# Attention with a two-layer network on one core: the lower parts of the first layer's results may go to VectorE or GpSimd in every group, and two of the attention's products get a wider planning margin

## Chip, cores and metric

One core of a Trainium2 chip. The metric is device time in microseconds, the median of the runs shown. The inputs are the reference's; the program is compiled with its whole order fixed, so what can change from one version to the next is which engine does an operation and where it stands in that engine's queue.

## What is computed

```python
# q, k, v: (4, 8, 768, 64); n_global = 8, n_local = 96
scores = scale * np.matmul(q, k.transpose(0, 1, 3, 2))
keep = is_global | is_local            # first 8 keys, and the last 96 up to the query
bias = -slopes[:, None, None] * dist[None, :, :]
scores = np.where(keep, scores + bias, -1000000000.0)
a = softmax(scores)                    # maximum, exp, sum + 1e-9
x = np.matmul(a, v).transpose(0, 2, 1, 3).reshape(3072, 512)
h = x @ w_in                           # 512 -> 2048
g = np.where(h > 0.0, h, np.exp(np.minimum(h, 0.0)) - 1.0)
out = g @ w_out                        # 2048 -> 512
```

## The kernel before

The 3072 rows are twelve **groups** of 256 rows (four batches of three). Each group has an attention part and a network part. The attention of a group is four **pairs** of heads (`pair`). In the groups 4 to 11 each head goes through `head`: for each of its two tiles of 128 queries a score product `s` (line 561), the softmax on VectorE and ScalarE (`pr`, lines 478, 480, 487, 488, 468), the transposes of the weights `t` (line 575), their split into a rounded upper half and the rest (`pt`, ScalarE line 287 and VectorE line 295), and the product with the values `pv` (line 587). Then VectorE adds the two halves to `x` (line 459), and `xh` and `xl` are the upper and lower parts of the group's rows. There is one bank for `t` and one for `pv`: the next transposes wait until VectorE has read the last `t`. The groups 0 to 3 take another way (`heads32`), which the change does not touch.

The network of a group is `moe`: for each of 16 slices of the hidden width, `up` makes h with twelve products of 256 columns (line 606), ScalarE and VectorE apply the nonlinearity (lines 612 to 614), ScalarE rounds it to the upper part `gh` (line 615, helper line 287), and the **lower part** `gl = e - gh` is a subtraction (line 616, helper line 295). `down` adds six products of 512 columns to the group's two outputs `o` (line 628): four with gh, two with gl. TensorE works on the network of one group while the attention of the next is prepared beside it.

The order of all this is no loop but a plan. `Plan.add` records each operation with the engines that may do it and their estimated costs (`dve(W, port=True)` is VectorE, `pool(W)` is GpSimd; `port` says that the operation takes the memory port that the two share), a due time, and a `slack`. `Plan.order` goes through them greedily: it takes, per engine, first what is ready, by due time. An operation with several engines is only given to one if no other would end sooner. The slack is a margin: an operation counts as ready only `slack` after its inputs from other engines,

```python
t = t + self.SEM + op.slack if of != e else t - self.LAT["PE"] if e == "PE" else t
at = max(at, f + self.SEM + 0.3 * op.slack)
```

and 0.3 of it after its buffer came free (second line). So a wider margin makes the plan put other work in between; the program itself waits on semaphores alone and does not add the margin. Before, the margin is 600 ns for the score products, the transposes and the value products of `head`. The subtraction for `gl` may go to either engine in the groups 0 to 2 and in the last group, and to GpSimd alone in the groups 3 to 10.

Of the kernel before, what the change touches and what calls it, by code (L numbers as in the profile page):

```python
# [20 lines left out]
W = NT * P  # L21
# [180 lines left out]
def pe(cols):  # L202
    return (("PE", cols * 0.47, False),)


def act(n, psum=False, extra=0.0):
    return (("ACT", (55 if psum else 97) + 0.834 * n + extra, False),)


def dve(n, fast=False, port=False):  # L210
    return (("DVE", (75 + 0.521 * n) if fast else (70 + 1.042 * n), fast or port),)


def pool(n, two=True):
    return (("POOL", (30 + 2.58 * n) if two else (50 + 1.1 * n), True),)


def sp():
    return (("SP", 450.0, False),)
# [21 lines left out]
class Kernel:  # L241
# [306 lines left out]
    def head(self, b, h, t0, j, qd, ql, ks, vd, pv, due, step):  # L548

        nc, p, slack = self.nc, self.plan, self.SLACK  # L550
        st = self.sb("st", "st", [P, 3, NT])
        prs = []
        for i in range(NT):
            lo = 0 if t0 + i else P
            n, c0 = 2 * P - lo, NG + i * (NG + P) + lo
            s = self.bank("s", "s", [P, 1, 2 * P])
            prs.append(self.sb("pr", "pr", [P, 2 * P]))

            def scores(e, i=i, s=s, lo=lo, n=n, c0=c0):
                for m, x in enumerate((qd, ql)):  # L560
                    nc.tensor.matmul(s.t[:, 0, lo:], x.t[:, j, i * P:(i + 1) * P], ks.t[:, j, c0:c0 + n], start=m == 0, stop=m == 1)  # L561

            p.add((("PE", 130.0 * n / P + 30, False),), scores, [qd, ql, ks], [s], due + i * step - 5000, slack=slack)
            self.softmax(b, h, t0 + i, s, 0, prs[i], st, i, due + i * step)
        self.inverse(st, due - 3500)
        for i, pr in enumerate(prs):
            d = due + i * step
            lo = 0 if t0 + i else P
            a0, n = lo // P, 2 * P - lo
            self.norm(pr, lo, st, i, d - 3000, False)  # L570
            tp = self.bank("t", "t", [P, 2, P])

            def transposes(e, pr=pr, tp=tp, a0=a0):
                for a in range(a0, 2):
                    nc.tensor.transpose(tp.t[:, a], pr.t[:, a * P:(a + 1) * P], self.ident.t)  # L575

            p.add((("PE", 75.0 * (2 - a0), False),), transposes, [pr], [tp], d - 2500, slack=slack)

            pt = self.sb("pt", "pt", [P, 2, 2, P], F32R)
            p.add(act(n, True), lambda e, pt=pt, tp=tp, a0=a0: self.copy(e, pt.t[:, a0:, 0], tp.t[:, a0:]), [tp], [pt], d - 2000)  # L580
            p.add(dve(n), lambda e, pt=pt, tp=tp, a0=a0: self.minus(e, pt.t[:, a0:, 1], tp.t[:, a0:], pt.t[:, a0:, 0]),
                  [tp, pt], [pt], d - 1500)

            def values(e, pt=pt, a0=a0, i=i):

                for a in range(a0, 2):
                    nc.tensor.matmul(pv.t[:, i].rearrange("p s w -> p (s w)"), vd.t[:, 2 * i + a, j].rearrange("p s d -> p (s d)"),  # L587
                                     pt.t[:, a].rearrange("p s w -> p (s w)"), start=a == a0, stop=a == 1)

            p.add((("PE", 122.0 * (2 - a0), False),), values, [vd, pt], [pv], d, slack=slack)  # L590

    def moe(self, rows, xh, xl, f0, f1, dues, step, part, X, last):
        nc, p, NFC, ws = self.nc, self.plan, self.NFC, self.ws
        acc = []
        G = {}

        def up(fc, d):
            w1 = ws[0][fc]  # L600
            h = self.bank("h", "h", [P, W])
            for n in range(3):
                def mm1(e, n=n, h=h, w1=w1):
                    s, x = ((HI, xh), (LO, xh), (HI, xl))[n]
                    for cc in range(self.NCC):
                        nc.tensor.matmul(h.t, w1.t[:, s, cc * P:(cc + 1) * P], x.t[:, cc],  # L606
                                         start=n == 0 and cc == 0, stop=n == 2 and cc == self.NCC - 1)
                p.add(pe(self.NCC * W), mm1, [w1, xl if n == 2 else xh], [h], d + n)
            ex = self.sb("e", "e", [P, W])
            gh, gl = self.sb("gh", "gh", [P, W], F32R), self.sb("gl", "gl", [P, W], F32R)  # L610

            p.add(act(W, True), lambda e: nc.scalar.activation(ex.t, h.t, AF.Relu, scale=-1.0), [h], [ex], d - 8000)  # L612
            p.add(act(W), lambda e: nc.scalar.activation(ex.t, ex.t, AF.Exp, scale=-1.0), [ex], [ex], d - 8000)  # L613
            p.add(dve(W), lambda e: nc.vector.scalar_tensor_tensor(ex.t, ex.t, -1.0, h.t, ALU.add, ALU.max), [h, ex], [ex], d - 8000)  # L614
            p.add(act(W), lambda e: self.copy(e, gh.t, ex.t), [ex], [gh], d - 8000)
            p.add((dve(W, port=True) if X or last else ()) + pool(W), lambda e: self.minus(e, gl.t, ex.t, gh.t), [ex, gh], [gl], d - 8000)
            G[fc] = gh, gl

        def down(fc, d):
            w2 = ws[1][fc]  # L620
            gh, gl = G.pop(fc)
            if not acc:
                acc.extend(self.bank(f"o{i}", "o", [P, self.DM]) for i in range(NT))
            for n in range(2):
                for i in range(NT):
                    def mm2(e, n=n, i=i):
                        for g, s in ((gh, HI), (gh, LO)) if n == 0 else ((gl, HI),):
                            nc.tensor.matmul(acc[i].t, g.t[:, i * P:(i + 1) * P], w2.t[:, s],  # L628
                                             start=fc == f0 and n == 0 and s == HI, stop=fc == f1 - 1 and n == 1)
                    ends = fc in (f0, f1 - 1)  # L630
                    p.add(pe(self.DM * (2 - n)), mm2, [w2, (gh, gl)[n]], [acc[i]],
                          d + (10 * i + n if ends else 10 * n + i))

        for fc in range(f0, f1):

            up(fc, dues[fc] - (1.3 * step if last and fc > NFC - 3 else 0.0))
            down(fc, dues[fc] + 2 * step)
        end = dues[f1 - 1] + 2 * step
        for i in range(NT):
            if f1 < NFC:  # L640
                if f0 == 0:

                    self.parted.append(p.add(act(self.DM, True), lambda e, i=i: self.copy(e, part.t[:, i], acc[i].t), [acc[i]], [part], end - 9000))
                else:
                    p.add(dve(self.DM), lambda e, i=i: nc.vector.tensor_tensor(part.t[:, i], acc[i].t, part.t[:, i], ALU.add),
                          [acc[i], part], [part], end - 9000)
                continue

            m = 2 if last and i == NT - 1 else 1
            n = self.DM // m  # L650
            for c in range(0, self.DM, n):
                ob = self.sb("io", "ob", [P, n])
                e, half = ("ACT", "DVE")[c // n], slice(c, c + n)
                cost = act(n, True) if e == "ACT" else dve(n)
                if f0 == 0:
                    p.add(cost, lambda e, i=i, ob=ob, half=half: self.copy(e, ob.t, acc[i].t[:, half]), [acc[i]], [ob], end - 9000)
                else:
                    p.add(dve(n), lambda e, i=i, ob=ob, half=half: nc.vector.tensor_tensor(ob.t, acc[i].t[:, half], part.t[:, i, half], ALU.add),
                          [acc[i], part], [ob], end - 9000)
                queue = nc.scalar if m > 1 and c == 0 else nc.sync  # L660
                p.add((("ACT", 450.0, False),) if queue is nc.scalar else sp(),
                      lambda e, i=i, ob=ob, half=half, queue=queue: queue.dma_start(self.out[rows + i * P:rows + (i + 1) * P, half], ob.t),
                      [ob], [], end, nbytes=P * n * 4)

    def build(self):
# [41 lines left out]
        for _, f in sorted(todo, key=lambda x: x[0]):  # L707
# [9 lines left out]
    EARLY = [dict(FIRST, rqv=FIRST["rqv"] + ["part0", "part1"], rk=FIRST["rk"] + ["qd0", "ql0"], pr=FIRST["pr"] + ["ks0"],  # L717
                  pt=FIRST["pt"] + ["vd0"], t=["t0", "h0"], s=["s0", "s1", "o0", "o1"], pv=["v0"]), dict(FIRST, whole=True), dict(FIRST, whole=True),
             {"rqv": ["rqv0", "ks0"], "rk": ["rk0", "qd0", "ql0"], "rows": True, "whole": True}, {}]
    SLACK = 600.0  # L720
    WARM = True
    SLOTS = {"rqv": ["rqv0"], "rk": ["rk0"], "qd": ["qd0"], "ql": ["ql0"], "ks": ["ks0"], "vd": ["vd0", "part0", "part1"],
             "s": ["s0", "s1"], "t": ["t0"], "pv": ["v0"], "h": ["h0", "h1"], "o0": ["o0"], "o1": ["o1"],
# [255 lines left out]
```

## Time and profile before

| | |
|---|---|
| median of 3 runs | 711.27 us (710.24 to 713.42) |
| profiled execution | 711.18 us, its span 709.4 us |
| TensorE products busy | 693.8 us, 98% of the span |
| TensorE weight loads busy | 615.0 us, 87% |
| VectorE busy | 517.3 us, 73% |
| ScalarE busy | 504.0 us, 71% |
| GpSimd busy | 246.5 us, 35% |
| chain that ended last | PE 71%, DVE 16%, DMA 6%, ACT 4% |

PE is TensorE, PEld its weight loads, DVE VectorE, ACT ScalarE, POOL GpSimd, SP the DMA queue. A matmul's shown time overlaps with that of the next, so a TensorE that reads as busy may still have lost time: that shows in the distance from one start to the next. Windows are microseconds from the start of the span.

### The profile page before, as it was taken

The page shows a single profiled execution, that of the slowest core. Times are in us where ns is not written, and L with a number is a line of the kernel's source. Part 1 is how long each engine was busy: PE and PEld are TensorE (multiplying, and loading weights), DVE is VectorE, ACT ScalarE, POOL GpSimd, SP SyncE. Part 2 cuts the span into 40 slices and gives each one's busy share as a digit, 9 for nine tenths or more (in the row PEclk, how much of TensorE's full clock was granted, in tenths as well). Part 3 has the DMA queues.
Part 4 walks back from the last instruction along what each step waited for, and adds up shares of the span by engine and source line. Part 5 has one row for each costly group of instructions (what it writes and reads, how often), then busy time and mean ns, then how long its engine had stood idle before and what let it go on. Part 6 is the DMA issues. An engine that isn't in the chain of part 4 may idle for free.

```text
span 709.4 us, 13834 instructions
## 1 busy us (share of the span) xinstructions
PE 693.8 (98%) x4701; PEld 615.0 (87%) x4701; DVE 517.3 (73%) x1571; ACT 504.0 (71%) x1463; POOL 246.5 (35%) x274
## 2 busy tenths in 40 slices
PE   9989999999999999999999999999999999999996
PEld 6768888889898989999989999999989989999895
DVE  6999999996658958856766875884783884884322
ACT  6989887774657758867767876876776785875442
POOL 2430543440023443433453452542443354332000
PEclk9999999999999999999999999999999999999999
DMA  8443960000233212312312222230331321210000
GB/s 322 176 127 132 419 274 24 1 24 1 76 105 94 82 54 83 107 54 84 107 54 83 80 81 64 73 106 31 107 83 40 107 71 51 84 54 1 31 1 34
DMA packets 22254, 63.49 MB, mean 89 GB/s; under 512 B 2592, under 2 KB 4896, under 8 KB 22176
## 3 DMA queue, kind: packets, MB, share of 16 engines
q1 hardware_dynamic: 21888, 62.40, 26.3%
q8 instruction: 39, 0.64, 0.4%
q14 instruction: 39, 0.32, 0.1%
q10 hardware_dynamic: 288, 0.13, 0.1%
HBM read 56.23 MB, written 6.29 MB: 88 GB/s over the span
## 4 chain that ended last, share of the span: by engine, by line
PE 71%; DVE 16%; DMA 6%; ACT 4%; issue 2%; SPq 1%; DVEq 0%; ACTq 0%
PE h L606 29%; PE o L628 29%; PE pv L587 4%; PE s L561 4%; DMA bits<-in_w_out_dram 4%; PE t L575 3%; DVE g L372 2%; DVE g L374 2%; DVE e L614 2%; DVE w L295 1%; DVE gl L295 1%; DVE pr L478 1%; DVE ks L295 1%; DMA rqv<-in_qkv_dram 1%; DVE pr L468 1%
## 5 line engine op out<-in xcount | busy, mean ns | idle before, releaser
L606 PEld LDWEIGHTS h<-xh,w 128*128 128x128 f32 x1536 | 228.2, 189 | 26.5 <-issue 1.0
L606 PE MATMUL h<-xh,w 128*128 128x256 f32 x1536 | 245.7, 283 | 0.3 <-DVE e L614 0.3
L628 PE MATMUL o<-w,gh 128*128 128x512 f32 x768 | 243.7, 399 | 1.3 <-DVE w L295 0.4
L295 POOL TENSOR_TENSOR gl<-e,gh 128x256 fp32r<-128x256 f32 x133 | 101.8, 765 | 263.5 <-ACT gh L287 253.8
L628 PEld LDWEIGHTS o<-w,gh 128*128 128x128 f32 x768 | 126.2, 189 | 15.2 <-ACT gh L287 2.8
L614 DVE SCALAR_TENSOR_TENSOR e<-e,h 128x256 f32<-128x256 f32 x192 | 80.0, 417 | 73.0 <-ACT e L613 64.5
L628 PE MATMUL o<-w,gl 128*128 128x512 f32 x384 | 133.0, 400 | 0.0
L612 ACT ACTIVATE e<-h 128x256 f32<-128x256 f32 x192 | 73.3, 382 | 74.6 <-PE h L606 67.4
L606 PE MATMUL h<-xl,w 128*128 128x256 f32 x768 | 123.6, 283 | 0.0
L287 ACT CAST gh<-e 128x256 fp32r<-128x256 f32 x192 | 77.4, 403 | 54.1 <-DVE e L614 53.1
L606 PEld LDWEIGHTS h<-xl,w 128*128 128x128 f32 x768 | 104.2, 189 | 0.3 <-issue 0.2
L478 DVE CUSTOM_DVE_ANT_0 pr<-s,tab 128x256 f32<-128x256 f32 (+1 forms) x192 | 73.4, 395 | 42.5 <-PE s L561 37.5
L480 ACT ACTIVATE pr<-pr,nmax 128x256 f32<-128x256 f32 (+1 forms) x192 | 93.6, 488 | 13.4 <-DVE nmax L478 12.7
L613 ACT ACTIVATE e<-e 128x256 f32<-128x256 f32 x192 | 80.1, 418 | 4.2
L369 POOL TENSOR_SCALAR g<-g 128x512 f32<-128x512 f32 x25 | 54.3, 2180 | 69.9 <-ACT g L367 65.2
L459 DVE TENSOR_TENSOR x<-pv,x 64x256 f32<-64x256 f32 x128 | 53.7, 419 | 21.3 <-ACT x L287 18.7
L628 PEld LDWEIGHTS o<-w,gl 128*128 128x128 f32 x384 | 63.7, 189 | 2.2
L468 DVE TENSOR_SCALAR pr<-pr,st 128x256 f32<-128x256 f32 (+1 forms) x159 | 62.2, 421 | 1.2
L287 ACT CAST pt<-t 128x256 fp32r<-128x256 f32 (+1 forms) x128 | 45.5, 355 | 20.9 <-PE t L575 20.3
L295 DVE TENSOR_TENSOR pt<-t,pt 128x256 fp32r<-128x256 f32 (+1 forms) x128 | 51.5, 402 | 11.6 <-ACT pt L287 10.8
L575 PE MATMUL t<-ident,pr 128*128 128x128 f32 x240 | 47.4, 273 | 2.8 <-DVE pt L295 2.5
L587 PE MATMUL pv<-pt,vd 128*128 128x256 f32 x240 | 49.5, 289 | 0.1
(92 smaller groups left out, 880.7 us busy)
## 6 DMA issues: line engine op xcount, KB each, us to landing
rqv<-in_qkv_dram SPq DMA_DIRECT2D x32, 512.0 KB, 3.5
rk<-in_qkv_dram SPq DMA_DIRECT2D x32, 400.0 KB, 3.2
bits<-in_w_in_dram SPq DMA_DIRECT2D x16, 512.0 KB, 9.0
bits<-in_w_out_dram SPq DMA_DIRECT2D x16, 512.0 KB, 9.7
rqv<-in_qkv_dram SPq DMA_DIRECT2D x16, 384.0 KB, 3.6
out_dram<-ob SPq DMA_DIRECT2D x23, 256.0 KB, 2.0
rk<-in_qkv_dram SPq DMA_DIRECT2D x16, 200.0 KB, 4.8
out_dram<-ob ACTq DMA_DIRECT2D x1, 128.0 KB, 2.6
```

The source lines that it names most:

```text
L287: self.nc.scalar.copy(out, x)
L295: self.on(e).tensor_tensor(out, x, y, ALU.subtract)
L468: self.nc.vector.tensor_scalar(out, x, sc, None, ALU.mult)
L478: p.add((("DVE", 158 + 1.042 * n, False),), lambda e: nc.vector.tensor_tensor_reduce(pr.t[:, lo:], s.t[:, m, lo:], tab, -(2.0 ** -(h + 1)) ...
L480: p.add(act(n, extra=200), lambda e: nc.scalar.activation(pr.t[:, lo:], pr.t[:, lo:], AF.Exp, bias=nm, scale=-1.0, accum_out=st.t[:, 0, i: ...
L575: nc.tensor.transpose(tp.t[:, a], pr.t[:, a * P:(a + 1) * P], self.ident.t)
L587: nc.tensor.matmul(pv.t[:, i].rearrange("p s w -> p (s w)"), vd.t[:, 2 * i + a, j].rearrange("p s d -> p (s d)"), pt.t[:, a].rearrange("p ...
L606: nc.tensor.matmul(h.t, w1.t[:, s, cc * P:(cc + 1) * P], x.t[:, cc], start=n == 0 and cc == 0, stop=n == 2 and cc == self.NCC - 1)
L612: p.add(act(W, True), lambda e: nc.scalar.activation(ex.t, h.t, AF.Relu, scale=-1.0), [h], [ex], d - 8000)
L613: p.add(act(W), lambda e: nc.scalar.activation(ex.t, ex.t, AF.Exp, scale=-1.0), [ex], [ex], d - 8000)
L614: p.add(dve(W), lambda e: nc.vector.scalar_tensor_tensor(ex.t, ex.t, -1.0, h.t, ALU.add, ALU.max), [h, ex], [ex], d - 8000)
L628: nc.tensor.matmul(acc[i].t, g.t[:, i * P:(i + 1) * P], w2.t[:, s], start=fc == f0 and n == 0 and s == HI, stop=fc == f1 - 1 and n == 1)
```

## The change

```diff
-            p.add((("PE", 75.0 * (2 - a0), False),), transposes, [pr], [tp], d - 2500, slack=slack)
+            p.add((("PE", 75.0 * (2 - a0), False),), transposes, [pr], [tp], d - 2500, slack=self.LATER)
...
-            p.add((("PE", 122.0 * (2 - a0), False),), values, [vd, pt], [pv], d, slack=slack)
+            p.add((("PE", 122.0 * (2 - a0), False),), values, [vd, pt], [pv], d, slack=self.LATER)
...
-            p.add((dve(W, port=True) if X or last else ()) + pool(W), lambda e: self.minus(e, gl.t, ex.t, gh.t), [ex, gh], [gl], d - 8000)
+            p.add(dve(W, port=True) + pool(W), lambda e: self.minus(e, gl.t, ex.t, gh.t), [ex, gh], [gl], d - 8000)
...
-    SLACK = 600.0
+
+    SLACK, LATER = 600.0, 1200.0
```

The margin of the transposes and of the value products goes from 600 to 1200 ns; that of the score products stays. The subtraction for `gl` may go to VectorE in every group. In the new order 176 of the 192 subtractions stand on VectorE and 16 on GpSimd; before it was 59 and 133. No instruction is added or left out on any engine. The order is the same up to the first moved subtraction.

GpSimd's order around the preparation of group 7 (`vd` are the split values of a pair, `xl` the lower part of a group's rows), before:

```order
L295 TENSOR_TENSOR gl_4922<-e_4879,gh_4909 128x256
L295 TENSOR_TENSOR gl_4966<-e_4929,gh_4954 128x256
L289 CAST vd_4984<-rqv_4926 128x4x2x64
L295 TENSOR_TENSOR vd_4984<-rqv_4926,vd_4984 128x4x128
L295 TENSOR_TENSOR gl_5049<-e_5002,gh_5032 128x256
L295 TENSOR_TENSOR xl_4724<-x_4986,xh_4713 128x256
L295 TENSOR_TENSOR gl_5094<-e_5058,gh_5087 128x256
```

and now:

```order
L295 TENSOR_TENSOR xl_4771<-x_4807,xh_4763 128x256
L289 CAST vd_4979<-rqv_4921 128x4x2x64
L295 TENSOR_TENSOR vd_4979<-rqv_4921,vd_4979 128x4x128
L295 TENSOR_TENSOR xl_4771<-x_4999,xh_4763 128x256
L289 CAST vd_5142<-rqv_5075 128x4x2x64
```

All subtractions for `gl` have left this stretch of GpSimd; `vd` and `xl` remain.

VectorE's order at the same place (pair 3 of group 6; the VectorE half of `pt` is the last reader of the single `t` bank, `ks` is the lower part of the next pair's keys, `ql` that of its queries), before:

```order
L295 TENSOR_TENSOR ks_5022<-rk_4902,ks_5022 64x800
L459 TENSOR_TENSOR x_4986<-pv_5024,x_4986 64x256
L478 ISA pr_5055,nmax<-s_5004,tab_69 128x256
L478 ISA nmax 128x1
L295 TENSOR_TENSOR pt_5047<-t_5041,pt_5047 128x128
```

and now:

```order
L437 SCALAR_TENSOR_TENSOR ql_5058<-rqv_4921,qd_5030 128x256 x2
L295 TENSOR_TENSOR gl_5069<-e_5023,gh_5056 128x256
L478 ISA pr_5079,nmax<-s_5018,tab_69 128x256
L478 ISA nmax 128x1
L295 TENSOR_TENSOR pt_5077<-t_5067,pt_5077 128x128
L295 TENSOR_TENSOR ks_5060<-rk_4903,ks_5060 64x800
```

The large subtraction for `ks` has moved from ahead of the `pt` that frees the bank to behind it, and a subtraction for `gl` now stands ahead of it.

TensorE's order where the network of group 6 ends and that of group 7 begins (`o` are the outputs of group 6; the first row that reads another `xh` is the first product of group 7), before:

```order
L606 MATMUL h_6036<-xl_4724,w_515_2263 128x256 x4
L628 MATMUL o_5333<-w_506_2253,gl_6023 128x512
L628 MATMUL o_5377<-w_506_2253,gl_6023 128x512
L561 MATMUL s_6060<-ks_5850,qd_5843 128x256
L561 MATMUL s_6060<-ks_5850,ql_5905 128x256
L628 MATMUL o_5333<-w_512_2313,gh_6044 128x512 x2
L606 MATMUL h_6068<-xh_5540,w_78_408 128x256 x4
L628 MATMUL o_5377<-w_512_2313,gh_6044 128x512 x2
```

and now, beginning with the row behind the last value product of group 7 (that row is `L587 MATMUL pv_6035<-pt_6033,vd_5665 128x256 x2`):

```order
L628 MATMUL o_5369<-w_512_2313,gh_6031 128x512 x2
L628 MATMUL o_5333<-w_512_2313,gl_6038 128x512
L628 MATMUL o_5369<-w_512_2313,gl_6038 128x512
L561 MATMUL s_6071<-ks_5861,qd_5837 128x256
L561 MATMUL s_6071<-ks_5861,ql_5876 128x256
L561 MATMUL s_6077<-ks_5861,qd_5837 128x256
L561 MATMUL s_6077<-ks_5861,ql_5876 128x256
L628 MATMUL o_5333<-w_518_2357,gh_6074 128x512 x2
L628 MATMUL o_5369<-w_518_2357,gh_6074 128x512 x2
L628 MATMUL o_5333<-w_518_2357,gl_6082 128x512
L628 MATMUL o_5369<-w_518_2357,gl_6082 128x512
L606 MATMUL h_6096<-xh_5558,w_78_408 128x256 x8
```

Before, the last value product of group 7 stood 8.7 us ahead of group 7's first product, and two slices of group 6 were still to be finished beside it; now eleven rows stand between the two, and group 6 is finished first. The place where group 9 gives way to group 10 has the same new order; at the other changes of group two slices still overlap.

## Rows read from the trace of the kernel before

**Rows 1.** The page, busy time of each engine.

```profile
PE 693.8 (98%) x4701; PEld 615.0 (87%) x4701; DVE 517.3 (73%) x1571; ACT 504.0 (71%) x1463; POOL 246.5 (35%) x274
```

**Rows 2.** Windows: stretch, length, busy us of PE, PEld, DVE, ACT, POOL; clock, DMA.

```profile
160.00:640.00 480.00, 477.10 (x3252) 434.41 (x3251) 344.77 (x1044) 344.26 (x1018) 182.22 (x219) 1.00 0.24 74
560.00:580.00 20.00, 20.00 (x142) 18.43 (x141) 18.00 (x56) 16.47 (x51) 9.56 (x11) 1.00 0.32 95
```

**Rows 3.** Timeline of TensorE, network alone: start us, length us, instruction.

```profile
655.43 0.64 PE L606 MATMUL h<-xh,w 128*128 128x256 f32 x4
655.90 0.62 PE L628 MATMUL o<-w,gh 128*128 128x512 f32 x2
656.36 0.63 PE L606 MATMUL h<-xh,w 128*128 128x256 f32 x4
```

**Rows 4.** Groups by line, 160 to 645 us: busy, mean ns | idle before, releaser.

```profile
L575 PE MATMUL t<-ident,pr 128*128 128x128 f32 x239 | 47.3, 273 | 2.8 <-DVE pt L295 2.5 <-DVE st L487 0.2
```

**Rows 5.** Timeline of TensorE at the first, the two longest and the last late transposes.

```profile
214.49 0.62 PE L628 MATMUL o<-w,gh 128*128 128x512 f32 x2
215.28 0.41 PE L575 MATMUL t<-ident,pr 128*128 128x128 f32 x2 [0.16 <-DVE st L487]
...
357.68 0.63 PE L606 MATMUL h<-xh,w 128*128 128x256 f32 x4
359.04 0.41 PE L575 MATMUL t<-ident,pr 128*128 128x128 f32 x2 [0.74 <-DVE pt L295]
...
525.44 0.63 PE L606 MATMUL h<-xh,w 128*128 128x256 f32 x4
527.09 0.41 PE L575 MATMUL t<-ident,pr 128*128 128x128 f32 x2 [1.02 <-DVE pt L295]
...
583.56 0.63 PE L628 MATMUL o<-w,gh 128*128 128x512 f32 x2
584.54 0.41 PE L575 MATMUL t<-ident,pr 128*128 128x128 f32 x2 [0.35 <-DVE pt L295]
```

**Rows 6.** Timeline of VectorE, ScalarE and GpSimd ahead of the wait at 359.04.

```profile
356.05 1.72 DVE L295 TENSOR_TENSOR ks<-rk,ks 64x800 fp32r<-64x800 f32 x1 [0.27 <-ACT ks L287]
358.61 0.29 DVE L295 TENSOR_TENSOR pt<-t,pt 128x128 fp32r<-128x128 f32 x1
...
357.06 0.25 ACT L287 CAST pt<-t 128x128 fp32r<-128x128 f32 x1
...
355.51 1.41 POOL L295 TENSOR_TENSOR vd<-rqv,vd 128x512 fp32r<-128x512 f32 x1
356.88 1.49 POOL L295 TENSOR_TENSOR gl<-e,gh 128x256 fp32r<-128x256 f32 x1
```

**Rows 7.** Groups by line and shape, whole span: the lower parts and their products.

```profile
L295 POOL TENSOR_TENSOR gl<-e,gh 128x256 fp32r<-128x256 f32 x133 | 101.8, 765 | 263.5 <-ACT gh L287 253.8 <-PE o L628 6.9 <-issue 2.4
L295 DVE TENSOR_TENSOR gl<-e,gh 128x256 fp32r<-128x256 f32 x59 | 26.3, 447 | 10.7 <-ACT gh L287 10.5
L628 PE MATMUL o<-w,gl 128*128 128x512 f32 x384 | 133.0, 400 | 0.0
L295 DVE TENSOR_TENSOR ks<-rk,ks 64x800 fp32r<-64x800 f32 x24 | 25.8, 1075 | 0.9 <-ACT ks L287 0.3
```

**Rows 8.** Timeline of TensorE: group 7's last value product, and its first network product.

```profile
421.79 0.40 PE L587 MATMUL pv<-pt,vd 128*128 128x256 f32 x2
...
430.68 0.64 PE L606 MATMUL h<-xh,w 128*128 128x256 f32 x4
```

**Rows 9.** Groups by line and shape: what lies between those two, and its rivals on ScalarE.

```profile
L480 ACT ACTIVATE pr<-pr,nmax 128x256 f32<-128x256 f32 x160 | 81.0, 507 | 9.2 <-DVE nmax L478 8.9
L287 ACT CAST gh<-e 128x256 fp32r<-128x256 f32 x192 | 77.4, 403 | 54.1 <-DVE e L614 53.1
L459 DVE TENSOR_TENSOR x<-pv,x 64x256 f32<-64x256 f32 x128 | 53.7, 419 | 21.3 <-ACT x L287 18.7
L287 ACT COPY x<-pv 64x256 f32<-64x256 f32 x64 | 23.5, 368 | 3.5 <-PE pv L587 2.0
L287 ACT CAST xh<-x 128x256 fp32r<-128x256 f32 x32 | 12.9, 402 | 4.2 <-DVE x L459 4.1
```

## The prediction

> **What bounds the kernel now.** I read the page's busy times first: TensorE's products are busy for 98% of the span [rows 1]. So a gain can only come from time that TensorE loses, and the question is how much that is and where. The windows say that from 160 to 640 us, where the network runs beside the attention of later groups, it is busy for 477.10 of 480 us [rows 2]. But that figure hides a part. In the network alone four products of 256 columns start 0.47 us before what follows them, and two of 512 columns 0.46 us, while each row is shown as 0.62 to 0.64 us long [rows 3]: the next product starts while the last is still shown. Hence I measure lost time as the distance from one start to the next, less that pace.
>
> Read so, the timeline shows late transposes. At 357.68 four products should be followed at 358.15, and the transposes start at 359.04: 0.89 us lost, of which the view shows 0.74 as idle. At 525.44 it is 1.18 us, at 214.49 0.33 us, at 583.56 0.52 us [rows 5]. After the first moved subtraction (about 210 us) I find thirteen such places: seven at transposes, 3.9 us together, and six at value products, 0.13 to 0.30 us each, 1.2 us together; 5.1 us in all. As a check, the transposes' group has 2.8 us of visible idle time, nearly all of it put down to VectorE's half of the split, `pt` [rows 4]; thirteen times the 0.16 us or so that a transpose's 273 ns hide behind the 0.11 us pace add about 2.1, and 2.8 + 2.1 = 4.9.
>
> Why are they late? Take 359.04. ScalarE cast its half of `pt` at 357.06, but VectorE came to the other half only at 358.61, because it sat in the subtraction for `ks` from 356.05 for 1.72 us [rows 6], where the mean of such a subtraction is 1.075 us [rows 7]. GpSimd was in its subtraction for `vd` from 355.51 for 1.41 us, and its next one, a `gl`, was shown for 1.49 us instead of its mean 0.765 [rows 6, 7]. The two engines held each other up, and the transposes' only bank came free late. The place at 527.09 is the same one three groups later.
>
> **What the change does, part by part.**
>
> *The moved subtractions.* The order has 133 - 16 = 117 fewer on GpSimd and as many more on VectorE. GpSimd loses 117 x 0.765 = 90 us, VectorE gains 117 x 0.447 = 52 us [rows 7]. On TensorE's path neither counts by itself: the product that uses `gl` never waited, with 0.0 us idle over 384 instructions [rows 7]; the order keeps the work between the up-projection and that product (median 6.7 us at the pace of rows 3, before and after). So I cost the move at nothing. The cover is VectorE's free time: 344.77 of 480 us are busy, and 52 more make 397, or 83% [rows 2]. Without that cover everything behind VectorE slips, which is a rival below.
>
> *Fewer meetings at the shared port.* The same move takes GpSimd's most frequent instruction away from VectorE's `ks`, `ql` and scaling. What it gives back cannot be read off as one row; it lies between nothing and the 0.65 us (1.72 - 1.075) that the longest `ks` paid [rows 6, 7], at each of the few places where this decides. I take it together with the next term.
>
> *The wider margins.* Every transposing step and every value product of groups 4 to 11 is put later behind its inputs. Counted in the order at the pace of rows 3, the least TensorE work between transposes and the value product that uses them goes from 1.77 to 2.34 us, and from the last score product to the transposes from 3.6 to 4.1 us (median 5.8 to 7.8). So at least about 0.5 us more stands in front of each. If each of the thirteen waits shrinks by just that, those of 0.89 and 1.18 us keep 0.4 and 0.7, and the rest nearly vanish: 1.2 us stays. If the late VectorE instruction is gone as well, nothing stays. At the place of rows 6 the new order has `ks` behind `pt`, but the work between one transposing step and the next there is 1.63 us instead of 1.87. I take the middle, 0.6 us left, so a **gain of 5.1 - 0.6 = 4.5 us**; both ends go into the range.
>
> *What is late next.* The later value products make the attention of a group end later. At group 7 its last value product started at 421.79 and the first network product followed at 430.68 [rows 8], 8.7 us behind its end. In the new order only 2.8 us of TensorE work lies between (three times two products of 512 with gh and four with gl, and two score steps: 6 x 0.23 + 4 x 0.23 + 4 x 0.12). In it `x` must be copied, added twice, and cast: 0.368 + 2 x 0.419 + 0.402 = 1.6 us [rows 9]. Ahead of or between these on the queues stand one exponential of the next group (0.507), one cast for gh (0.403) and one `gl` on VectorE (0.447) [rows 7, 9]: 1.36 us if none overlaps, together 3.0 against 2.8. So at most about 0.2 us late by these rows, plus the handing over between engines that I do not see here. Behind it, group 6's work is used up, so a late `gh` of group 7 has less beside it. I take 0.3 us here and as much at group 10, where the order is the same; below is nothing, above 1 us each. **Cost 0.6 us.** The other changes of group keep 3.7 to 5.1 us and overlap with the last two slices; no cost.
>
> Sum: 711.18 (the profiled execution, whose span is 709.4) - 4.5 + 0.6 = 707.3 us; the median of the runs is 0.09 us above that execution, too little to move the figure: **707.3 us**.
>
> **A rule against this change.** The row at 356.88 shows GpSimd's `gl` stretched to 1.49 us beside `ks` [rows 6]. A subtraction of two tiles on VectorE can meet GpSimd's `vd` in just the way that `ks` did. The Trainium skill (Perfetto Trace Analysis, Optimizing Scalar/DVE Operations) says that VectorE and GpSimd share a read port, so that moving operations between them may not help; SBUF — State Buffer (Who interferes with whom) adds that a VectorE instruction with two inputs in that memory contends with a GpSimd one that reads it, and the loser waits in full. By that rule VectorE's 117 new instructions are new losers, and the trace agrees that such meetings occur. It is the first rival.
>
> **The rivals.**
>
> 1. *The waits come back elsewhere.* Each late `pt` now has on average one more `gl` ahead of it, 0.447 us [rows 7], which eats most of the 0.5 us of new margin; `vd` still holds the port. Then thirteen waits of mean 0.39 us keep 0.39 - 0.5 + 0.447 = 0.34, 4.4 us, and the time is 711.2 - 5.1 + 4.4 + 0.6 = 711.1 us; with half of the waits so affected it is about 709. For it: VectorE is busy for 18.00 of 20 us in a dense window, and 52 us over 480 add 2.2 there [rows 2]. Against: GpSimd is busy for 90 us less, so that there are fewer instructions to meet.
>
> 2. *Slower: VectorE falls behind in each group, and the next group's first product waits.* In the dense stretches 18.0 + 2.2 is over 20 [rows 2]. If VectorE ends a group's attention some 3 us late, each of the eight changes of group loses what its lead (4.0, 3.9, 3.7, 2.8, 4.3, 3.7, 2.8 and 5.1 us of TensorE work in the order) less the 1.6 us chain does not cover: 0.6 + 0.7 + 0.9 + 1.8 + 0.3 + 0.9 + 1.8 + 0 = 7.0 us. With half of the old waits left, 711.2 - 2.6 + 7.0 = 715.6 us. It decides from a lag of about 1.2 us at groups 7 and 10 and 2.1 at the others. Against it: 397 of 480 us still leave thin stretches in which to catch up.
>
> **How the numbers follow.** Forecast, 705.4 to 708.8 us: 0.60. The upper bound of the gain, 5.1 + 0.6 from the terms above, gives the lower end. First rival, 708.8 to 711.5: 0.28. Second rival: 0.07. The remaining 0.05 is for what I have not seen, on either side. A measurement of this kernel can tell about 0.5% from no change, 3.6 us, so faster means below 707.7. My forecast lies just past that line: of its 0.60 I put 0.44 below, and 0.03 of the rest, together 0.47 faster; 0.16 + 0.28 + 0.01 = 0.45 the same; 0.08 slower. The range leaves out the second rival, the first one's upper end and the unseen: 705.4 to 710.8.
>
> **What would show it.** Right: GpSimd near 157 us busy, VectorE between 550 and 569 us; TensorE's idle time ahead of the transposes under 1 us from 200 to 640 us; `ks` means nearer 1.0 than 1.075 us. The steps fail if the transposes still wait for `pt` at a dozen places (rival 1), or if the first product of a group waits for `xh` by more than 1 us at more than two groups (rival 2). The prediction as a whole is wrong if the 5.1 us of waits are gone and the time is not: then I have missed what replaced them.

## The result, and the profile after the change

The changed kernel takes **716.43 us** (median of 6 runs, 714.34 to 718.22); the kernel before takes 711.67 us beside it (6 runs, 710.24 to 713.42). The ratio is **1.0058**, with a 95% interval of 1.0040 to 1.0075: slower by 0.58%, some 4 us (the two medians lie 4.8 us apart). Forecast were 707.3 us, and a range up to 710.8. The profiled execution is the fastest of the six, 714.34 us with a span of 712.2, against a span of 709.4 before, so the trace shows 2.8 us of the loss and not all of it. Ratios here and below are of the fast executions alone; one of e1's and one of e10's were far slower (1362 and 1127 us).

The page's busy times, and the chain that ended last by engine (it was PE 71%, DVE 16% before):

```profile
PE 694.2 (97%) x4701; PEld 613.1 (86%) x4701; DVE 553.9 (78%) x1688; ACT 505.9 (71%) x1463; POOL 151.1 (21%) x157
...
PE 63%; DVE 26%; ACT 4%; DMA 3%; issue 3%; SPq 0%; DVEq 0%; ACTq 0%
```

GpSimd lost 95 us and VectorE gained 37 against [rows 1], and the chain now runs through VectorE for a quarter of the span. The same two windows as in [rows 2] (stretch, length, then busy us of PE, PEld, DVE, ACT and POOL):

```profile
160.00:640.00 480.00, 475.19 (x3229) 430.31 (x3228) 375.62 (x1140) 342.57 (x1004) 90.19 (x106) 1.00 0.24 74
560.00:580.00 20.00, 19.18 (x133) 17.50 (x132) 18.46 (x51) 14.97 (x44) 5.49 (x7) 1.00 0.24 69
```

TensorE is busy for 1.9 us less of the same 480. VectorE has 375.62 us where the prediction counted 397, and the window from 560 to 580 us, the dense one before, holds 18.46 of 20, not 20.2. The groups by line from 160 to 645 us (busy us, mean ns | idle before, releaser) show where TensorE stands still; the first row answers to [rows 4], and the third is the value products before the change:

```profile
L575 PE MATMUL t<-ident,pr 128*128 128x128 f32 x234 | 46.5, 274 | 3.6 <-DVE pt L295 3.4
L587 PE MATMUL pv<-pt,vd 128*128 128x256 f32 x232 | 49.5, 289 | 1.2 <-DVE x L459 0.9
...
L587 PE MATMUL pv<-pt,vd 128*128 128x256 f32 x236 | 48.6, 289 | 0.1
```

The transposes idle for 3.6 us instead of 2.8, and the value products, 0.1 us before, for 1.2. Counted as in the prediction (from one start to the next, less the pace of that pair of lines; from 205 us on, places of more than 0.11 us), it is 18 places and 7.5 us, where it was 13 places and 5.1 us. The waits were to shrink to 0.6 us; they grew.

The subtractions, as groups by line and shape over the whole span, answer to [rows 7]:

```profile
L295 DVE TENSOR_TENSOR gl<-e,gh 128x256 fp32r<-128x256 f32 x176 | 82.4, 469 | 24.8 <-ACT gh L287 23.0
L295 DVE TENSOR_TENSOR ks<-rk,ks 64x800 fp32r<-64x800 f32 x24 | 24.6, 1027 | 2.0 <-ACT ks L287 1.3
```

and the view of the tile `gl` adds the shortest, median and longest in ns:

```profile
L295 DVE TENSOR_TENSOR gl<-e,gh x176: 402/424/1556, 48.7 to 703.8; 128x256 fp32r<-128x256 f32 x176
```

The mean of `ks` fell from 1075 to 1027 ns: fewer meetings, as hoped. The busy time of `gl` on VectorE grew from 26.3 us [rows 7] to 82.4, by 56, and that of VectorE as a whole by 37, so all its other work takes 19 us less. But now a `gl` on VectorE can be the one that is held up, for up to 1556 ns. One late place of the new kernel in its timeline (start, length, instruction; the stretch ends at the idle transposes):

```profile
404.65 1.30 POOL L295 TENSOR_TENSOR vd<-rqv,vd 128x512 fp32r<-128x512 f32 x1
...
404.79 1.43 DVE L295 TENSOR_TENSOR gl<-e,gh 128x256 fp32r<-128x256 f32 x1
...
406.78 0.99 DVE L295 TENSOR_TENSOR ks<-rk,ks 64x800 fp32r<-64x800 f32 x1
...
407.09 0.38 PE L575 MATMUL t<-ident,pr 128*128 128x128 f32 x2
...
408.72 0.42 DVE L614 SCALAR_TENSOR_TENSOR e<-e,h 128x256 f32<-128x256 f32 x1
409.17 0.43 DVE L459 TENSOR_TENSOR x<-pv,x 64x256 f32<-64x256 f32 x1
409.63 0.42 DVE L295 TENSOR_TENSOR pt<-t,pt 128x256 fp32r<-128x256 f32 x1
...
410.11 0.44 PE L575 MATMUL t<-ident,pr 128*128 128x128 f32 x2 [0.76 <-DVE pt L295]
```

`gl` starts 0.14 us behind `vd` and takes 1.43 us instead of 0.42. VectorE carries the delay on through `ks` and the rest of its queue, comes to `pt` only at 409.63, and the next transposes, whose weights `pr` were long ready, stand still for the one bank that `pt` has to read first. Either half of the change could be to blame here: the `gl` on VectorE, or the order that the margins made.

### The profile page after: what moved, and what is told of

Its sections match the earlier page's. It is cut to its first block, busy times and chain, and to the rows that moved or that the text cites. A ratio compares the mean times of both kernels' runs of the same rounds, so it can differ in the third digit from the quotient of the medians.

```text
span 712.2 us, 13526 instructions
## 1 busy us (share of the span) xinstructions
PE 694.2 (97%) x4701; PEld 613.1 (86%) x4701; DVE 553.9 (78%) x1688; ACT 505.9 (71%) x1463; POOL 151.1 (21%) x157
## 4 chain that ended last, share of the span: by engine, by line
PE 63%; DVE 26%; ACT 4%; DMA 3%; issue 3%; SPq 0%; DVEq 0%; ACTq 0%
PE o L628 26%; PE h L606 26%; PE pv L587 3%; PE s L561 3%; PE t L575 3%; DVE gl L295 2%; DVE pr L478 2%; DMA bits<-in_w_out_dram 2%; DVE e L614 2%; DVE pr L468 2%; DVE x L459 2%; DVE g L372 2%; DVE g L374 2%; DVE pt L295 2%; DVE ks L295 2%
## 5 line engine op out<-in xcount | busy, mean ns | idle before, releaser
L295 DVE TENSOR_TENSOR gl<-e,gh 128x256 fp32r<-128x256 f32 x176 | 82.4, 469 | 24.8 <-ACT gh L287 23.0
L468 DVE TENSOR_SCALAR pr<-pr,st 128x256 f32<-128x256 f32 (+1 forms) x159 | 59.7, 405 | 0.9
L289 POOL CAST vd<-rqv 128x512 fp32r<-128x512 f32 (+1 forms) x32 | 19.0, 593 | 186.4 <-DMA rqv<-in_qkv_dram 155.0
L295 POOL TENSOR_TENSOR xl<-x,xh 128x256 fp32r<-128x256 f32 x32 | 24.4, 761 | 136.3 <-ACT xh L287 136.3
L587 PE MATMUL pv<-pt,vd 128*128 128x256 f32 x240 | 51.2, 289 | 1.2 <-DVE x L459 0.9
```

The source lines that it names most:

```text
L295: self.on(e).tensor_tensor(out, x, y, ALU.subtract)
L468: self.nc.vector.tensor_scalar(out, x, sc, None, ALU.mult)
```

## The experiments

All are timed against the kernel before on the same chip in the same batch. The waits are counted in each one's profiled execution, as above; where a pair of lines is rare its pace is less sure, which can move a count by one or two places.

| run | what it is | median us | ratio [95%] | places, us of waits |
|---|---|---|---|---|
| before | | 711.7 to 712.2 | 1 | 13, 5.1 |
| after | the whole change | 716.43 | 1.0058 [1.0040, 1.0075] | 18, 7.5 |
| e1 | moved subtractions alone | 712.26 | 0.9999 [0.9983, 1.0015] | 10, 3.4 |
| e2 | both margins alone | 715.96 | 1.0056 [1.0037, 1.0076] | 16, 6.4 |
| e3 | after, `vd` set | 711.03 | 0.9976 [0.9957, 0.9994] | 16, 3.1 |
| e4 | before, `vd` set | 709.39 | 0.9955 [0.9938, 0.9973] | 8, 1.8 |
| e5 | after, whole margin behind banks | 711.05 | 0.9988 [0.9976, 1.0001] | 5, 3.7 |
| e6 | before, whole margin behind banks | **709.39** | **0.9970 [0.9958, 0.9981]** | 11, 2.2 |
| e7 | transposes' margin alone | 718.62 | 1.0095 [1.0081, 1.0109] | 26, 9.2 |
| e8 | value products' margin alone | 711.92 | 0.9997 [0.9985, 1.0009] | 11, 3.6 |
| e9 | e7, whole margin behind banks | 711.27 | 0.9991 [0.9980, 1.0002] | 10, 3.6 |
| e10 | transposes' margin 900 | 716.76 | 1.0064 [1.0045, 1.0083] | 24, 7.2 |
| e11 | e1, whole margin behind banks | 710.66 | 0.9984 [0.9967, 1.0001] | 10, 3.2 |
| e12 | e6, `vd` on either engine | 710.06 | 0.9979 [0.9966, 0.9991] | 11, 2.9 |

A straight line through the fourteen, median = 706.7 + 1.31 x waits, leaves at most 1.7 us at any point (correlation 0.97). So these waits are the right thing to look at, and a microsecond of them in a trace stands for a little more than one in the time. The line sets medians against one trace each; within the traces alone, from the 1300th product (at about 196 us) on, the slope is 1.19 and the correlation 0.96.

### Which half of the change (e1 to e4)

Three theories. P: VectorE's longer queue, and its meetings with GpSimd, make the loss. M: the margins make it. C: the plan fell out badly by chance. In e1 and e2 one half of the change is undone in the kernel after; in e3 and e4 the subtraction that makes the lower halves of the values on GpSimd only sets them to zero, in the same place of the order, so it reads nothing (the lower halves of v are left out). It is also shorter: 0.53 us in the mean instead of 1.31 (the instructions of 512 columns).

```diff
# e1: the margins as before, gl on either engine
-    SLACK, LATER = 600.0, 1200.0
+    SLACK, LATER = 600.0, 600.0
# e2: gl as before, the margins wider
-            p.add(dve(W, port=True) + pool(W), lambda e: self.minus(e, gl.t, ex.t, gh.t), [ex, gh], [gl], d - 8000)
+            p.add((dve(W, port=True) if X or last else ()) + pool(W), lambda e: self.minus(e, gl.t, ex.t, gh.t), [ex, gh], [gl], d - 8000)
# e3 (in the kernel after) and e4 (in the kernel before)
-        p.add(pool(nv), lambda e: self.minus(e, vv()[:, :, 1:3, :], v32()[:, v0:], vv()[:, :, 0::3, :]),
+        p.add(pool(nv), lambda e: nc.gpsimd.memset(vv()[:, :, 1:3, :].bitcast(F32), 0.0),
```

> The subtractions for gl may go to VectorE in every group, both margins stay at 600 ns (the order puts 186 of 192 on VectorE). Theory P (VectorE's queue: a subtraction for gl on VectorE stands behind GpSimd's vd at the shared port and delays the pt behind it): slower than before by 3 to 5 us, 714 to 717 us, with late transposes waiting for pt as in the changed kernel. Theory M (the wider margins make the loss, by pushing the attention's steps together at the end of a group): within 1.5 us of before, 710 to 713 us. Theory C (any new order has its own tight places): either, without a pattern shared with the changed kernel.

> Margins of the transposes and value products at 1200 ns, gl where it was before (133 on GpSimd, 59 on VectorE). P: no slower than before, 707 to 711 us, since each transposing step has about 0.5 us more work ahead of it and VectorE is no fuller. M: slower, 713 to 717 us. C: either.

> The changed kernel in the same order, but GpSimd writes zeros for the lower half of the split values vd instead of subtracting, so that it reads nothing there; the lower halves of v are left out of the result. P: the 1.3 us during which VectorE's subtractions stood behind vd are gone, and 3 us or more of the waits with them: 711 to 713.5 us. M and C: the order is the same, so the waits stay: within 1 us of the changed kernel, 715 to 717 us.

> The kernel before with the same zeros in place of the subtraction for vd (the lower halves of v are left out). P: the two longest waits (0.89 and 1.18 us, where ks stood behind vd) and some short ones go: 708.5 to 710 us, a smaller gain than e3's. M and C: no more than 1 us.

e2 is as slow as the whole change, and e1 is no slower than before. So **the loss comes with the margins**, in full and without the moved subtractions; P falls as to the `gl` on VectorE. The waits for engines on TensorE from 205 to 645 us (us in total, times, longest), of e1 and then of e2:

```profile
PE t L575 <- DVE pt L295: 1.1, 2, 0.6
PE pv L587 <- DVE x L459: 0.4, 1, 0.4
PE o L628 <- ACT gh L287: 0.2, 1, 0.2
```

```profile
PE t L575 <- DVE pt L295: 3.2, 8, 0.5
PE pv L587 <- DVE x L459: 0.2, 1, 0.2
```

e1 with 186 subtractions on VectorE has fewer waits for `pt` than the kernel before (1.1 against the 2.5 of [rows 4]); e2, with VectorE's load as before, has more. Yet e1 gains no time: its trace has 1.7 us less of waits, and 11 more of the short gaps told of at the end, worth 1.1 us.

In e3 and e4, though, it is P that forecast right and M that failed: M, which saw the waits in the order alone, expected 715 to 717 us for e3 and a gain of no more than 1 us for e4, and P 711 to 713.5 and 708.5 to 710. Measured are 711.03 and 709.39. So GpSimd's subtraction for `vd` has a part in most of the waiting: 4.4 of the 7.5 us go with it after, and 3.3 of the 5.1 before. Most of the loss needs both, the margins' order and GpSimd's `vd` beside it: with `vd` set the kernel after is 0.2% behind the kernel before (0.9976 against 0.9955), with the subtraction 0.6%. After, the groups by line of the transposes go from 3.6 us idle to this:

```profile
L575 PE MATMUL t<-ident,pr 128*128 128x128 f32 x236 | 46.7, 274 | 0.7 <-DVE pt L295 0.6
```

The ratio falls by 0.0082 (5.8 us) after, and by 0.0045 (3.2 us) before. The engine that makes VectorE late is the same in both; what differs is how much of that lateness reaches TensorE. That the gain is the reading's, and not that of the shorter instruction, is not shown by these two runs alone; the part on rival 1 below has a measure of it. Theory C was left open.

### Whose margin, and what is waited for (e5 to e8)

What e1 to e4 leave is why a wider margin makes waits. Theory B: the waits are for the single bank of `t` or of `pv`, which VectorE frees, and not for operands. The wider margin pushes steps behind operands that were never late, while behind the release of a bank the plan leaves only 0.3 of it, so the turn-arounds of the banks get tight. Theory R: any wider margin draws steps away from where they cost nothing. e5 (on the kernel after) and e6 (on the kernel before) change one factor; e7 and e8 are the kernel before with one of the two new margins.

```diff
# e5, e6
-                        at = max(at, f + self.SEM + 0.3 * op.slack)
+                        at = max(at, f + self.SEM + op.slack)
# e7: the transposes alone (LATER is 1200)
-            p.add((("PE", 75.0 * (2 - a0), False),), transposes, [pr], [tp], d - 2500, slack=slack)
+            p.add((("PE", 75.0 * (2 - a0), False),), transposes, [pr], [tp], d - 2500, slack=self.LATER)
# e8: the value products alone
-            p.add((("PE", 122.0 * (2 - a0), False),), values, [vd, pt], [pv], d, slack=slack)
+            p.add((("PE", 122.0 * (2 - a0), False),), values, [vd, pt], [pv], d, slack=self.LATER)
```

> The changed kernel, but the plan adds the whole margin, not 0.3 of it, behind the release of a buffer or bank (one factor in the plan's order). Theory B (the waits are for the transposes' only bank, which VectorE's pt frees; the widened margin guards the operands, which were not late): waits for pt nearly vanish and the time falls by 2 us or more against the changed kernel, to 711 to 714 us, less what the shorter lead at the changes of group costs (2.2 to 3.0 us of TensorE work in the order). Theory R (any wider margin draws a pair's steps out, so that more of them run into the next pair's on VectorE): no gain or slower, 716 to 719 us.

> The kernel before, margins of 600 ns, gl as before, with the whole margin behind the release of a bank. B: waits for pt fall from 2.5 us of idle time to under 1, and the time by 2 to 3.5 us, 708.5 to 710.5 us. R: slower than before, 713 to 716 us.

> Margin of 1200 ns for the transposes alone; value products at 600 ns, gl as before. If the transposes' margin makes the loss: 714 to 717 us, as with both. If the value products' margin does: 711 to 713 us. If the two only hurt together: both single ones within 1.5 us of before.

> Margin of 1200 ns for the value products alone; transposes at 600 ns, gl as before. If the value products' margin makes the loss (it sends the additions to x later, into the next pair's softmax on VectorE): 714 to 717 us. If the transposes' margin does: 711 to 713 us.

The transposes' margin alone is worse than the whole change, and 718.62 us is above the 714 to 717 that were expected; the value products' alone is nothing, and on top of the other it takes some of the loss back (1.0095 in e7, 1.0056 in e2). In e7 most of the waiting has moved from the `t` bank to the `pv` bank; its waits on TensorE, and one of the longest places in its timeline:

```profile
PE pv L587 <- DVE x L459: 4.2, 9, 0.7
PE t L575 <- DVE pt L295: 0.7, 3, 0.3
```

```profile
417.29 0.48 PE L587 MATMUL pv<-pt,vd 128*128 128x256 f32 x2
417.34 0.99 DVE L295 TENSOR_TENSOR ks<-rk,ks 64x800 fp32r<-64x800 f32 x1
...
419.93 0.89 DVE L437 SCALAR_TENSOR_TENSOR ql<-rqv,qd 128x256 fp32r<-128x256 f32 x1
...
420.33 0.63 PE L628 MATMUL o<-w,gl 128*128 128x512 f32 x2
...
421.13 0.43 DVE L459 TENSOR_TENSOR x<-pv,x 64x256 f32<-64x256 f32 x1
...
421.70 0.48 PE L587 MATMUL pv<-pt,vd 128*128 128x256 f32 x2 [0.74 <-DVE x L459]
```

The value product of 417.29 fills the bank. VectorE adds the last of it to `x` only at 421.13, behind `ks`, `ql` and what else stands in its queue, and the next value product starts at 421.70, as soon as that is done: 0.90 us later than the pace allows.

With the whole margin behind banks neither `t` nor `pv` is waited for in e5, and the loss of 0.58% is gone. What is left there are three waits of about 1 us at other banks, the two of h, which have no margin of their own:

```profile
PE h L606 <- DVE e L614: 2.9, 3, 1.0
```

e6 makes the kernel before faster by 0.30%, the best complete version that I ran, and its visible waits for `pt` go from 2.5 us to this:

```profile
PE t L575 <- DVE pt L295: 0.2, 1, 0.2
```

R falls as the main reason with e5: the margins there are as wide as in the slow kernels. A small cost of them is not excluded, since e5 is at 0.9988 and e6 at 0.9970.

The turn-around itself can be counted. From the last product of a transposing step to the end of the `pt` that frees its bank it is 1.39 us in the median before, 1.59 after, 1.60 in e2 and 1.68 in e7. The cover, TensorE's work at its pace from there to the next transposing step, did not shrink in the median: 1.99 us before, about 2.1 in the other three. Step by step, 36 of the 127 covers are shorter after than before, 68 longer. Steps that start less than 0.15 us behind that release, hence possibly held by it, are 11 of 128 before, 16 after, 17 in e2, 22 in e7 and 3 in e5. At the 16 after, the turn-around is longer than at the same step before in 13 cases, the cover shorter in 9; in e7 it is 17 and 9 of 22. So the steps are late mostly because VectorE comes to `pt` later in the new orders, and only in part because the steps moved together. Why VectorE comes later is not shown. In e5 and e9 the shortest cover is 2.1 us, against 1.2 before, 1.6 after and 1.4 in e7: the whole margin behind the bank leaves VectorE more time.

The count of such steps does not tell a good order from a bad one by itself: it is 17 in e6, the fastest kernel, and 19 in e8, which loses nothing. What tells them apart is how long TensorE waits in all: 2.2 and 3.6 us in these two, 7.5 after and 9.2 in e7.

### Theory B once more, the size, and two candidates (e9 to e12)

```diff
# e9: e7, and e11: e1, each with
-                        at = max(at, f + self.SEM + 0.3 * op.slack)
+                        at = max(at, f + self.SEM + op.slack)
# e10: e7 with
-    SLACK, LATER = 600.0, 1200.0
+    SLACK, LATER = 600.0, 900.0
# e12: e6 with
-        p.add(pool(nv), lambda e: self.minus(e, vv()[:, :, 1:3, :], v32()[:, v0:], vv()[:, :, 0::3, :]),
+        p.add(dve(nv, port=True) + pool(nv), lambda e: self.minus(e, vv()[:, :, 1:3, :], v32()[:, v0:], vv()[:, :, 0::3, :]),
```

> The transposes alone with a margin of 1200 ns, which was 0.95% slower than the kernel before, and now the whole margin also stands behind the release of a bank (it was 0.3 of it). Theory B (the waits are for the single bank of the transposes or of the value products, and the wider margin only postponed steps whose operands were never late): the value products' waits for VectorE's additions to x (4.2 us visible there) fall below 1.5 us and the time is 708 to 713, a ratio of 0.995 to 1.001. Theory R (any wider margin draws a step away from where it costs nothing): still 715 to 719, 1.005 to 1.010. Theory C (the planner's order is another draw each time): anything from 708 to 719, with no link between waits and time.

> The transposes' margin halfway, 900 ns, the 0.3 behind banks as it was. Theories B and R, in both of which the loss grows with the margin: between the kernel before and the run with 1200, so 713 to 717, a ratio of 1.002 to 1.007, with 6 to 8 us of waits. Theory C: no order by size, as likely below 711 or above 718 as between.

> The moved subtractions alone, with the old margins, and the whole margin of 600 ns behind the release of a bank. Theory B: the move costs nothing by itself and the bank's margin takes the waits of 3.4 us to about 1, so 708 to 710.5, a ratio of 0.995 to 0.998, as for the kernel before with the same bank margin or slightly below. Theory P (the move's load on VectorE costs time): above that kernel, 710.5 to 714.

> The kernel before with the whole margin behind banks, and the subtraction for the lower half of the values, which met VectorE's subtractions at the shared port, may go to VectorE too. If the meetings at the port make what is left of the waits: 706.5 to 709, a ratio of 0.993 to 0.9965, with fewer waits than 1.9 us. If VectorE's own longer queue takes their place: 709.4 to 712.

e9 is the plainest test: e7 was the slowest kernel of all, and the bank's margin takes it from 1.0095 to 0.9991. None of its steps follows a release within 0.15 us, and the waits on `t` and `pv` are gone from the view:

```profile
PE s L561 <- DVE ks L295: 0.9, 1, 0.9
PE h L606 <- DVE e L614: 0.7, 1, 0.7
PE o L628 <- ACT gh L287: 0.2, 1, 0.2
```

e10 lies between 600 and 1200 ns as forecast (1, 1.0064, 1.0095), which speaks against chance alone; but its waits are not those of e7:

```profile
PE o L628 <- ACT gh L287: 1.8, 3, 0.9
PE pv L587 <- DVE pt L295: 0.5, 2, 0.3
PE pv L587 <- DVE x L459: 0.3, 1, 0.3
PE t L575 <- DVE st L487: 0.2, 1, 0.2
```

So the amount follows the size, while the place does not: the plan is new each time, and most of the visible waits in e10 are for operands and not for banks, ScalarE's `gh` and the `pt` of value products. That part B does not explain.

e11 (710.66) fell at the edge between what B and P expected. Its interval overlaps that of e6, so a small cost of the moved subtractions on top of that order, up to a microsecond or so, is neither shown nor excluded. In e12 27 more instructions went to VectorE, and it is no faster than e6 (0.9979 against 0.9970): moving `vd` does not do what leaving out its reads did in e4. Its waits are again for `pt`, 0.8 us.

## Why the prediction was wrong

**What bounds the kernel: right.** The time went with TensorE's waits, as the line through the fourteen kernels shows, and with the kind of waits that the prediction found. The two spans differ by 2.8 us; waits (7.5 - 5.1 = 2.4 us) and short gaps (0.8 us) come to slightly more than that.

**The moved subtractions cost nothing: right.** e1 gives 0.9999. GpSimd came out at 151 us and VectorE at 554, about as told, and the products that read `gl` have 0.0 us of idle time from 160 to 645 us.

**The wider margins: the step that failed**, and with the wrong sign. It read: "So at least about 0.5 us more stands in front of each. If each of the thirteen waits shrinks by just that". The 0.5 us were counted between a step and its operands (from score product to transposes, from transposes to value product). But nearly all of the waiting at transposes was put down, in the same text, to `pt`, and so to the only bank; what covers that is the work from one transposing step to the next. The prediction had that number for one place (1.63 us instead of 1.87) and let it count only as a reason to take the middle. In front of the bank the change adds 0.3 x 0.6 = 0.18 us of margin at most by the planner's line. What the runs showed in place of the 0.5 us: the cover from one transposing step to the next grew by 0.1 us in the median, and VectorE's turn-around by 0.2. Instead of a gain of 4.5 us the margins alone cost 0.56% (e2), the transposes' alone 0.95% (e7).

**What is late next, 0.6 us at groups 7 and 10: not seen.** In the new trace no first product of a group waits for `xh`. The lower end of the range takes 0.6 us more than the waits for a gain; by the prediction's own terms the largest gain is the 5.1 us with no cost, so 706.1 us and not 705.4.

**Rival 1** was right in its name and not in its reason. The waits did come back, but not from one more `gl` ahead of each `pt`: e1 has those without a loss, and e2 has the loss without those. Its price, at most 711.1 us, was too small by 5 us as well. The rule that stood beside it holds all the same. The Trainium skill (SBUF — State Buffer, Who interferes with whom) says that a VectorE instruction contends with a GpSimd one that reads that memory when it has two inputs there, and not with one that only writes. The trace agrees: from 160 us on, `gl` on VectorE is 421 ns in the mean where GpSimd runs nothing, 729 ns in the 25 cases where it does, 1556 at the longest; in e3 the five that run beside GpSimd's setting of `vd` alone take 422 ns in the mean, the longest, 995, runs beside an `xl` too, and the loss is gone. **Rival 2** did not occur: its 715.6 us lie near the measured time by luck, since no group's first product was late.

What is shown: the margins make the loss, the transposes' above all; a whole margin behind the banks takes it back in two kernels (e5, e9) and makes the kernel before faster (e6); and so does leaving out GpSimd's reading of `vd` (e3). What stays open is why VectorE comes later to `pt` under the wider margins, and why a given plan is late at one step and not at another, of which e10 is the reminder.

## What to carry to other kernels

Before a margin is widened, ask of each wait whether it is for an operand or for a buffer: a margin behind operands does nothing by itself for a step that waits for its only bank, and the new order that it makes can bring the bank's reader later. Count the cover from one use of the buffer to the next, not from input to use, and set it against the time that the reader takes. And where a planner has one number for both, try the one behind the buffers first; here that was one factor, and 0.3% faster than the tuned kernel.

## What the runs showed of the hardware that I had not expected

Which VectorE instructions GpSimd holds up is sharp. After, from 160 us on, the normalisation of 256 columns (line 468) takes 346 ns in the mean alone and 736 beside GpSimd, `gl` 421 and 729, `ks` of 800 columns 990 and 1287; the nonlinearity (line 614) 417 and 416, the additions to `x` 420 and 419, the `pt` of 256 columns 418 and 420. The last three have a bank of the products' results among their inputs. So `pt` itself is not slowed here: where it is late, the delay comes from what stands ahead of it.

TensorE also loses many gaps of 0.04 to 0.11 us, at which the views name no releaser: 155 from 205 us on before (12.7 us), 167 after (13.5), 166 in e1 (13.8), 151 in e9 (12.6). What makes them is open. Before, 39 of the 155 stand within four products behind a separate semaphore instruction in TensorE's stream, where 13% of all products do; in e9 it is 7 of 151, against 9%, and the gaps are as many.

The traces also differ where their programs do not. TensorE's order is the same in all fourteen up to 212 us, and still its 300th product starts between 48.9 and 52.0 us. In seven traces (e3, e4, e6, e7, e9, e10, e12) the granted clock falls from 1.00 to 0.50, 2.4 to 1.2 GHz, for some 3 to 7 us from about 40 us on; in the others it is 1.00 there. The windows of the kernel before, and then of e7 (columns as in [rows 2]):

```profile
38.00:40.00 2.00, 0.66 (x4) 0.42 (x4) 1.97 (x10) 1.79 (x7) 0.33 (x1) 1.00 0.40 157
40.00:46.00 6.00, 5.66 (x50) 4.84 (x50) 5.53 (x21) 5.97 (x19) 2.97 (x2) 1.00 0.36 102
...
38.00:40.00 2.00, 0.66 (x4) 0.42 (x4) 1.97 (x8) 1.87 (x7) 0.26 (x1) 0.80 0.39 151
40.00:46.00 6.00, 5.81 (x31) 4.47 (x32) 4.29 (x15) 4.11 (x12) 2.24 (x1) 0.50 0.27 61
```

In both, TensorE was busy for 0.66 of the 2 us from 38 to 40. By the 300th product e7 is 2.2 us behind, so of the 7.9 us by which its span is longer that part is not the margins'; the waits, counted from 205 us on, hold none of it. Nor does it make e7's verdict: the four of its executions with a mean clock of 0.998 or 0.999 still take 718.0 to 719.4 us.
